# Replanning a fused sparse-attention and FFN kernel: DMA modelled as one stream, loads timed from need, fewer pairs on TensorE

## The chip, the cores and the metric

The kernel runs on one core of a Trainium2 chip. The metric is the device time of one execution in microseconds (us). Runs come in rounds, each with the kernel before beside the other on the same chip. "Fast" and "slow" are the states of an execution; here one is called slow when it is over 1.5% above the fastest of the same kernel. A median given below is of all runs.

The engines are PE (TensorE; PEld is its weight load), DVE (VectorE), ACT (ScalarE), POOL (GpSimd) and SP (which here mostly issues DMA). "Granted clock" is the share of TensorE's full clock in a stretch.

## The reference

Block-sparse attention over 4 batches and 8 heads of 768 tokens with 64 features, then a gated convolutional feed-forward part (FFN):

```python
scores = q @ k.T / 8
mask   = near_diagonal | first_and_last_block | sampled_blocks      # blocks of 32 tokens
x      = softmax(where(mask, scores, -1e9)) @ v                     # heads side by side: [4, 768, 512]
h      = maximum(x @ w_in, 0)                                       # [4, 768, 1024]
conv   = sum(conv_w[k] * shift(h, k - 1) for k in range(3))         # along the tokens
out    = (h * sigmoid(conv)) @ w_out                                # [4, 768, 512] float32
```

Inputs and outputs are float32; the kernel computes in bfloat16.

## The kernel before

The work is cut into 16 *pairs* (two heads of one batch) and 8 *halves* (384 tokens of one batch, all heads). Each pair's q and k are loaded by GpSimd's queue into `nat`, transposed so that the features lie on partitions, and copied by DVE into a slot `et`/`ot`. The first six pairs are transposed on TensorE. The others go through a DMA transpose into `tmp`:

```python
NSLOT = 6
NPE = 6                                   # pairs 0..5 on TensorE
...
t0 = op({"SP": 1.3}, xp(0), due - 8, [lq], alloc=tb, uses=[nb], lat=TLAT)     # DMA transpose of q
t1 = op({"SP": 1.3}, xp(1), due - 8, [lk], uses=[nb, tb], lat=TLAT)           # and of k, nat -> tmp
ce = op({"DVE": 0.5}, put(ET, 0), due, [t0, t1, slot_first.get(P - 1)], ...)  # et <- tmp
co = op({"DVE": 0.5}, put(OT, 64), due, [ce], uses=[slot_b[P], tb])           # ot <- tmp
```

Scores are TensorE matmuls into `st`; one exponential on ACT (`pt<-st`, 144 of them, each 1.04 us) takes eight blocks of 128x128; eight matmuls per exponential group multiply with v into `av`; DVE normalises (`xtok<-av`, 32 times), and a transpose gives `xT`, the input of the FFN. In the FFN TensorE multiplies (`mix<-xT,winb`), ACT or DVE applies the ReLU, DVE does the three multiplies and two adds of the convolution (`m<-hE`), ACT the tanh, DVE the gate, TensorE the output product. Half n's FFN runs while half n+1's attention does.

The order of all this is not written down. The kernel *declares* operations, each with the engines that may do it, a duration, a priority, its predecessors, a latency and its buffers; a list scheduler in the kernel then plans, while the program is being built, an order for each engine. `lat` of an operation is how long the planner believes its result takes to arrive. Twelve further passes re-plan, with priorities from the way back through the last plan:

```python
XLAT, TLAT = 3.908, 9.2201                # believed landing of xT's and tmp's transposes
PASSES = 12
...
def backward(self, order):                # priorities from the distance to the end
    ...
    for o, t in zip(order, end):
        o.prio = -t
        o.outs = []
        for b in o.allocs:
            b.index = None
            b.pool.holders = []           # o.start and o.end keep their old values

def run(self, passes):
    order = self.forward()
    for _ in range(passes):
        self.backward(order)
        order = self.forward()
    return order
```

Each engine executes its order strictly: one that reaches a copy whose transpose hasn't landed waits, whatever else stands behind (the profile after shows DVE do so for 8.71 us). Loads of later pairs were started at fixed times (`load_u`, as `earliest`). The mask rows of slots 2 to 5 were copied by DMA.

The softmax here doesn't subtract the row's maximum and nothing guards it: scores larger than these inputs give would overflow.

## Time and profile before

| | before |
|---|---|
| time, median of 3 | 215.12 us (215.08 to 215.75) |
| span of the profiled execution | 214.9 us (a fourth execution, of 216.58 us), mean granted clock 0.999 |
| busy DVE / PE / ACT | 189.7 / 198.8 / 182.1 us |
| attention ends (32nd normalisation starts) | 187.0 us |
| tail behind it | 27.9 us |

The prediction shows the busy table, the slices and the stretches. The granted clock in 40 slices, from the page (9 is 0.9 or more):

```profile
PEclk9999999999999999999999999999999999999999
```

The DMA transposes of q and k, from the DMA view, with the count and the median time from issue to landing in us:

```profile
tmp<-nat SPq DMA_TRANSPOSE x20, 6.5
```

There are two transposes for each of ten pairs, 20 in all. The 6.5 us needs care: the trace shows the landing of only 4 of the 20 (6.0 to 6.9 us), and the first of these 4 was issued at 52.1 us. The records of DMA packets cover the others. Each transpose into `tmp` moves 768 packets of 256 bytes and each into `xT` 384, and 20 x 768 + 27 x 384 = 25,728 is all that the trace has of this size. If the queue works them off in order, the transpose issued at 38.84 us, the first into `tmp`, began its last packet at 48.96 us, 10.1 us after its issue.

And the stretches, cut at the last normalisation of this execution, with busy us of PE, PEld, DVE, ACT, POOL, then granted clock, DMA share (packets of an engine overlap in time, so it can pass 1) and GB/s:

```profile
31.00:187.00 156.00, 149.48 (x2087) 117.20 (x2102) 147.64 (x415) 146.94 (x178) 56.09 (x128) 1.00 0.78 111
187.00:214.90 27.90, 22.76 (x119) 11.25 (x119) 22.20 (x65) 12.40 (x23) 6.03 (x14) 0.99 0.27 104
```

DVE is the third busy number. It idles 156.0 - 147.64 = 8.4 us in the middle and 27.9 - 22.20 = 5.7 us in the tail.

### The profile page before, as it was taken

The numbers are of one execution on the slowest core, as the hardware profiler recorded it, in microseconds if no ns is written. First come the engines' busy times: TensorE is split into PE (matmuls) and PEld (weight loads), VectorE is DVE, ScalarE is ACT, GpSimd is POOL, SyncE is SP. The second block draws the span as 40 slices with busy tenths as digits, with TensorE's granted clock in tenths as the row PEclk, the third lists the DMA queues.
The fourth block names the chain that finished last, engine by engine and source line by source line (L and its number), as shares of the span: only waits on it lengthen the run. The fifth ranks groups of instructions, "written<-read, shape, count | busy, mean of one in ns | idle before, by whom it ended". The sixth has DMA issues, their size and how long they took to land.

```text
span 214.9 us, 6588 instructions
## 1 busy us (share of the span) xinstructions
PE 198.8 (92%) x2579; PEld 150.4 (70%) x2596; DVE 189.7 (88%) x541; ACT 182.1 (85%) x227; POOL 81.8 (38%) x174
## 2 busy tenths in 40 slices
PE   7996999997999979999989999989999999998992
PEld 4785878886677857788768667667786787554441
DVE  6865627999989999479999999999999999999972
ACT  4595999999989989999998799989999999674541
POOL 8993414625505540446375302431241012443300
PEclk9999999999999999999999999999999999999999
DMA  6999994999999997899996993001110230022223
GB/s 170 152 177 204 199 203 61 142 154 134 190 136 212 150 119 80 148 146 213 168 136 106 129 204 107 18 20 62 59 23 21 71 116 21 18 98 101 99 98 146
DMA packets 50520, 25.84 MB, mean 120 GB/s; under 512 B 36321, under 2 KB 47353, under 8 KB 50489
## 3 DMA queue, kind: packets, MB, share of 16 engines
q0 software_dynamic: 18464, 11.14, 43.7%
q1 hardware_dynamic: 31592, 13.75, 31.6%
q10 hardware_dynamic: 432, 0.52, 0.7%
q8 instruction: 20, 0.33, 0.6%
q14 instruction: 12, 0.09, 0.2%
HBM read 23.08 MB, written 6.29 MB: 137 GB/s over the span
## 4 chain that ended last, share of the span: by engine, by line
DVE 59%; PE 15%; DMA 10%; ACT 6%; issue 5%; POOL 2%; SPq 1%; ACTq 0%; DVEq 0%; POOLq 0%
DVE m L753 19%; DVE m L759 10%; DVE hE L742 7%; PE st L678 6%; ACT pt L685 5%; DVE gT L781 5%; DVE xtok L631 5%; DMA nat<-in_k_dram 4%; DMA tmp<-nat 4%; PE mix L799 4%; DVE tn L772 3%; PE av L705 2%; DMA o2s<-in_q_dram 2%; DVE o2s L424 2%; PE st L799 2%
## 5 line engine op out<-in xcount | busy, mean ns | idle before, releaser
L685 ACT ACTIVATE pt<-st 128x1024 bf16<-128x1024 f32 x144 | 141.8, 1039 | 8.5 <-PE st L678 7.2
L705 PE MATMUL av<-vt,pt 128*128 128x65 bf16 x1152 | 57.9, 193 | 1.9 <-DVE vt L519 1.4
L753 DVE TENSOR_SCALAR m<-hE,cw 128x384 bf16<-128x384 bf16 x192 | 56.9, 346 | 0.2
L705 PEld LDWEIGHTS <-pt 128*128 128x128 bf16 x1152 | 50.4, 97 | 6.2 <-issue 1.7
L729 PE MATMUL mix<-xT,winb 128*128 128x384 bf16 x240 | 48.1, 325 | 1.9 <-DVE hE L742 1.1
L829 POOL COPY hE<-hE 128x254 bf16<-128x254 bf16 x32 | 18.4, 575 | 74.7 <-DVE hE L742 51.0
L799 PE MATMUL mix<-woutb,gT 128*128 128x512 bf16 x151 | 41.0, 379 | 2.4 <-DVE gT L781 1.6
L678 PE MATMUL st<-ot 88*128 88x128 bf16 (+1 forms) x224 | 42.5, 234 | 0.5 <-ACT pt L685 0.2
L678 PE MATMUL st<-et,ot 88*128 88x128 bf16 (+1 forms) x224 | 42.5, 234 | 0.1
L678 PE MATMUL st<-et 88*128 88x128 bf16 (+1 forms) x208 | 40.7, 239 | 1.7 <-ACT pt L685 1.7
L678 PEld LDWEIGHTS <-ot 88*128 88x128 bf16 x448 | 34.5, 97 | 10.1 <-issue 0.9
L678 PE MATMUL st<-ot,et 88*128 88x128 bf16 (+1 forms) x208 | 40.7, 239 | 0.7 <-ACT pt L685 0.4
L678 PEld LDWEIGHTS <-et 88*128 88x128 bf16 x416 | 32.3, 97 | 9.9 <-issue 3.3
L759 DVE TENSOR_TENSOR m<-m 128x768 bf16<-128x768 bf16 x64 | 35.1, 554 | 0.1
L769 ACT ACTIVATE tn<-m 128x768 bf16<-128x768 bf16 x32 | 27.7, 866 | 5.5 <-DVE m L759 5.4
L729 PEld LDWEIGHTS <-winb 128*128 128x128 bf16 x256 | 22.1, 97 | 13.1 <-issue 2.7
L799 PEld LDWEIGHTS <-gT 128*128 128x128 bf16 x200 | 16.5, 98 | 15.5 <-DVE gT L781 3.1
L742 DVE TENSOR_SCALAR hE<-mix 128x384 bf16<-128x384 f32 x37 | 20.2, 548 | 3.9 <-PE mix L729 3.8
L781 DVE TENSOR_TENSOR gT<-tn,hE 128x768 bf16<-128x768 bf16 x32 | 17.9, 562 | 0.1
L631 DVE TENSOR_TENSOR xtok<-av,rcp 128x384 bf16<-128x384 f32 x32 | 17.6, 549 | 0.3
L492 POOL DMA_DIRECT2D vn<-in_v_dram x16 | 11.9, 743 | 10.4 <-DVE vt L519 8.7
L830 POOL COPY hE<-hE 128x254 bf16<-128x254 bf16 x32 | 15.3, 479 | 0.0
(76 smaller groups left out, 168.7 us busy)
## 6 DMA issues: line engine op xcount, KB each, us to landing
out_dram<-o2s SPq DMA_DIRECT2D x23, 256.0 KB, 2.2
vn<-in_v_dram POOLq DMA_DIRECT2D x16, 192.0 KB, 6.2
nat<-in_q_dram POOLq DMA_DIRECT2D x15, 192.0 KB, 7.3
nat<-in_k_dram POOLq DMA_DIRECT2D x15, 192.0 KB, 6.4
winb<-in_moe_w_in_dram POOLq DMA_DIRECT2D x2, 512.0 KB, 12.2
woutb<-in_moe_w_out_dram POOLq DMA_DIRECT2D x2, 512.0 KB, 9.5
xT<-xtok SPq DMA_TRANSPOSE x27, 8.8
o2s<-in_k_dram ACTq DMA_DIRECT2D x2, 192.0 KB
```

Of the source, the lines that this page charges most:

```text
L631: nm = op({"DVE": 0.475}, lambda e: nc.vector.tensor_tensor(out=xtok_t[xk.index].rearrange("p c h d -> p h c d"), in0=o_of()[:, :, :, 0:64 ...
L678: nc.tensor.matmul(out=st_t[stb.index][:, 128 * x:128 * (x + n_)], lhsT=QK[kc % 2][s][0:88, 1, hh, kc // 2, :], rhs=QK[par][s][0:88, 0, hh ...
L685: e_op = op({"ACT": t_act(1024)}, lambda e, stb=stb, ptb=ptb: nc.scalar.activation(out=pt_t[ptb.index], in_=st_t[stb.index], func=AF.Exp, ...
L705: nc.tensor.matmul(out=av_t[av_buf[(n, P % 4)].index][:, off:off + 65], lhsT=pt_t[ptb.index][:, 128 * x:128 * x + 128], rhs=VT[P % NSLOT][ ...
L729: nc.tensor.matmul(out=tiles[hb.index][:, 0:384], lhsT=winb[:, fc, 128 * ffc:128 * ffc + 128], rhs=xT_t[xt_buf[n].index][:, fc, :], start= ...
L742: nc.vector.tensor_scalar(out=dst, in0=src, scalar1=0.5, scalar2=0.0, op0=ALU.mult, op1=ALU.max)
L753: nc.vector.tensor_scalar(out=m_t[cb.index][:, slot, o0:o1], in0=src, scalar1=w, scalar2=None, op0=ALU.mult)
L759: nc.vector.tensor_tensor(out=m[:, 0], in0=m[:, 0], in1=m[:, 1], op=ALU.add)
L769: th = op({"ACT": 0.745}, lambda e: nc.scalar.activation(out=tn_t[cb.index], in_=m_t[cb.index][:, 0], func=AF.Tanh, bias=0.0, scale=0.5), ...
L781: nc.vector.tensor_tensor(out=o, in0=t, in1=h, op=ALU.mult)
L799: nc.tensor.matmul(out=acc()[:, 0:o1 - o0], lhsT=gT_t[gb.index][:, ffc, 128 * c:128 * c + 128], rhs=woutb[:, ffc, o0:o1], start=(ffc == 0) ...
L829: nc.gpsimd.tensor_copy(out=h[:, f0:f0 + 2, 1:128], in_=h[:, f0:f0 + 2, 384:511])
```

## The change

The intent is a better plan: the planner counts every DMA on one shared stream (`DQ`) instead of giving each a private latency; loads begin 12 us ahead of need (`AHEAD`), read from the last plan; an engine may hold back up to 0.1 us for more urgent work (`PATIENCE`); four pairs stay on TensorE instead of six; mask rows go to DVE; one slot, one conv buffer and some FFN tiles are saved. All in one diff, cut to what matters (`...` marks cuts):

```diff
-FLEX = 0.0345
+FLEX = 0.054174241888482536
+PATIENCE = {"PE": 0.1, "ACT": 0.06768420072847306, "DVE": 0.002812048423731589}
...
-                    k = (s, o.prio, o.key)
+                    k = (max(s, t + PATIENCE.get(e, 0.0)), o.prio, o.key)
...
+        span = max(o.end for o in order)
         for o, t in zip(order, end):
             o.prio = -t
+            if o.ahead is not None:
+                o.earliest = span - t - o.ahead
             o.outs = []
+            o.start = o.end = None
...
-    NSLOT = 6
-    NPE = 6
+    NSLOT = 5
+    WIDE = ()
+    AHEAD = 12.0
+    NPE = 4
...
-    XLAT, TLAT = 3.908, 9.2201
+    XLAT, TLAT = 3.9296133203668684, 1.0
...
-    PASSES = 12
+    PASSES = 9
...
+    def sp_dma(fn, sp, dur, prio, deps, lat, alloc=None, uses=(), by="SP"):
+        i_ = op({by: sp}, fn, prio, deps, lat=0.1, alloc=alloc, uses=uses)
+        return op({"DQ": dur}, None, prio, [i_], lat=lat, uses=list(uses) + ([alloc] if alloc else []))
...
-            elif s == 1:
-                m[s] = op({"DVE": 0.58}, rows_by(t[s], t[0]), T(4.5 * s) - 2.5, [m[0]])
-            else:
-                m[s] = op({"SP": 0.46}, rows_to(t[s], t[0]), T(4.5 * s) - 6, [m[0]], lat=6.0,
-                          earliest=T(18 + 2 * s) if s > 3 else 0.0)
+            else:
+                m[s] = op({"DVE": 0.58}, rows_by(t[s], t[0]), T(4.5 * s) - 2.5, [m[0]])
...
-            t0 = op({"SP": 1.3}, xp(0), due - 8, [lq], alloc=tb, uses=[nb], lat=TLAT)
-            t1 = op({"SP": 1.3}, xp(1), due - 8, [lk], uses=[nb, tb], lat=TLAT)
+            t0 = sp_dma(xp(0), 1.25, 1.1, due - 8, [lq], TLAT, alloc=tb, uses=[nb])
+            t1 = sp_dma(xp(1), 1.25, 1.1, due - 8, [lk], TLAT, uses=[nb, tb])
...
-        xtr[(n, hp)] = op({"SP": 1.25}, tr, due - 5, [nm], lat=XLAT, uses=[xk] + us, alloc=al)
+        xtr[(n, hp)] = sp_dma(tr, 1.2, 0.8, due - 5, [nm], XLAT, uses=[xk] + us, alloc=al)
```

Left out: the same treatment of loads and stores, three conv buffers made two, the tanh written back into the conv buffer, batch-wide FFN tiles, other tuned offsets.

## The prediction

> **What bounds the kernel now.** I read the page's busy table first, then the table by stretch of time, then the groups, the chain that ended last, and the DMA landings. The page's head, its busy table and its slices:
>
> ```profile
> PE 198.8 (92%) x2579; PEld 150.4 (70%) x2596; DVE 189.7 (88%) x541; ACT 182.1 (85%) x227; POOL 81.8 (38%) x174
> ...
> PE   7996999997999979999989999989999999998992
> PEld 4785878886677857788768667667786787554441
> DVE  6865627999989999479999999999999999999972
> ACT  4595999999989989999998799989999999674541
> ...
> DMA  6999994999999997899996993001110230022223
> ```
>
> Three engines lie within 17 us of each other, so no single one explains the 215 us. The slices show where they are loose: DVE (VectorE) is loose in the first eight slices (to about 40 us) and around 85 us; the DMA engines are near full for the first 125 us and nearly empty after. I cut the trace at the points where this changes. Columns are busy us of each engine in the stretch, granted clock, DMA share and GB/s:
>
> ```profile
> 0.00:31.00 31.00, 26.52 (x376) 21.90 (x377) 19.83 (x63) 22.80 (x28) 19.65 (x32) 1.00 1.15 183
> 31.00:42.00 11.00, 11.00 (x173) 9.43 (x173) 8.63 (x22) 10.25 (x12) 5.12 (x12) 1.00 0.86 118
> 42.00:80.00 38.00, 34.79 (x512) 28.07 (x514) 37.12 (x104) 36.01 (x42) 17.24 (x34) 1.00 1.27 153
> 80.00:100.00 20.00, 19.90 (x292) 15.99 (x293) 15.56 (x44) 18.98 (x24) 6.22 (x13) 1.00 1.11 137
> 100.00:187.60 87.60, 84.39 (x1118) 63.89 (x1124) 86.93 (x251) 81.86 (x104) 27.51 (x71) 1.00 0.48 84
> 187.60:215.00 27.40, 22.16 (x116) 11.07 (x117) 21.60 (x63) 12.25 (x22) 6.03 (x14) 0.99 0.28 106
> ```
>
> 187.6 us is where the last attention output is normalised. DVE's idle time is 31.0 - 19.8 = 11.2 us in the start, 2.4, 0.9, 4.4, 0.7, and 5.8 in the tail. So from 42 us DVE is solid but for 80 to 100 us, where TensorE is (19.90 of 20). In the tail DVE runs without a gap to 208.3 us; then 6.6 us remain for the last output matmuls, the copy out and the store. The chain of waits says the same by share:
>
> ```profile
> DVE 59%; PE 15%; DMA 10%; ACT 6%; issue 5%; POOL 2%; SPq 1%; ACTq 0%; DVEq 0%; POOLq 0%
> ```
>
> The kernel is a start of some 31 us in which little but attention and loading runs, then 177 us in which DVE is the bound with one hole (80 to 100), then the closing 6.6 us.
>
> **What the Trainium skill says.** "Perfetto Trace Analysis", section "Identifying the Most-Contended Engine", takes occupancy as a fair measure for Vector and Scalar and not for matmuls; I therefore lean on DVE's 99% in 100 to 187.6 us and distrust TensorE's 96%. The trace agrees in part: eight attention-output matmuls count 0.41 us in the timeline, though the next kind begins 0.24 us after the first of them. The same page, "Optimization Strategy", says regimes with different limits may gain from interleaving; the hole at 80 to 100 us is such a regime. "DMA: Bandwidth & Descriptors", "Issuing engines are not separate DMA queues", has all queues run on the same 16 engines; the trace agrees: the two big queues take 43.7% and 31.6% of them, and the transposes of xtok land after 2.3 to 8.8 us. "VectorE: DVE Perf Modes", "Why PSUM operands drop a tier", says a PSUM source is slower per element; the groups agree: 768 elements from PSUM take about as long as 1536 from SBUF.
>
> ```profile
> L539 DVE COPY ot<-mix 64x768 bf16<-64x768 bf16 x12 | 6.7, 559 | 0.2
> L424 DVE COPY ot<-tmp 64x1536 bf16<-64x1536 bf16 x10 | 5.8, 580 | 0.3
> L424 DVE COPY et<-et 24x1536 bf16<-24x1536 bf16 x1 | 0.8, 758 | 0.0
> ```
>
> **The change, part by part.** I compared the static order of instructions of both kernels, engine by engine; it has counts and places and no time. Most of the diff (two conv buffers for three, batch-wide tiles for h and the gate, the tanh written into the conv buffer) changes no count: the wide path is switched off, so each engine does the same convolution in the same sizes.
>
> 1. *Four pairs on TensorE instead of six.* Pairs 4 and 5 now go through the DMA transpose. TensorE loses 24 transposes; six in a row took 0.49 us in the chain, so about 2 us. DVE loses 8 copies from PSUM (8 x 0.55 = 4.4 us) and gains 4 from SBUF (4 x 0.58 = 2.3 us). These stood at 36 to 45 us, where DVE is filling up: 2.1 us less on the path. Cost: four more DMA transposes at 20 to 35 us.
>
> 2. *Mask rows copied by DVE instead of DMA.* With 5 slots for 6, eight DMAs of 72 KB go; six copies of 24x1536 come (6 x 0.76 = 4.5 us). In the static order all six stand before the first FFN work, thus in the start with its 11.2 us of idle DVE. I count them as hidden. They free the queue of 6 x 72 KB, issued at 7.6 to 12 us, just ahead of a load of k issued at 11.27 us that took 8.96 us and is on the chain. ScalarE lost 3.1 us to scores between 10 and 31 us; I give this part 0.5 to 1 us.
>
> 3. *Balance of DVE and ScalarE.* DVE takes 3 more ReLUs (3 x 0.47 us, its spacing in the chain = 1.4 us) and one output copy less (0.6 us): +0.8 us on DVE; ScalarE gets about 1 us less.
>
> 4. *The sum on DVE.* Total: +4.5 - 4.4 + 2.3 + 0.8 = +3.2 us, so near 193 us busy. But of it +4.5 us (masks) and 1.2 us (pair 4's copies, now ahead of the FFN) fall into the start. After about 31 us there remains 189.7 - 19.8 = 169.9 us before, and 169.9 + 3.2 - 5.7 = 167.4 us after: 2.5 us less on the bound.
>
> 5. *Planner: one DMA stream, loads timed from need, patience.* No count changes, only order. It can only win by closing idle time: DVE's after 31 us and before the tail is 2.4 + 0.9 + 4.4 + 0.7 = 8.4 us. The new order does move FFN work: at the eighth normalisation 22 of the 192 multiplies stand ahead in both, but the first ones come a pair earlier (6 instead of 2 by the fifth). Behind the last attention output stand 104 output and 36 input matmuls of the FFN where it was 94 and 32. At their spacing in the timeline (0.217 and 0.163 us) that is 10 x 0.217 + 4 x 0.163 = 2.8 us of TensorE moved into the tail, and DVE's tail gains 6 multiplies, a gate, an add-one, less one ReLU: 6 x 0.24 + 0.47 + 0.27 - 0.47 = 1.7 us. So attention should end about 6 us earlier, and the tail be about 2 us longer. I credit 2 of the 8.4 us of idle as recovered; this is my choice, because TensorE bounds part of the hole.
>
> Sum: 2.5 us (work off the bound) + 0.5 (start) + 2.0 (idle recovered) = 5.0 us; less about 0.4 us for new waits on the transposes. 215.1 - 4.6 = **210.5 us**.
>
> **Rivals.**
> *The hole is only moved, nothing recovered.* For it: TensorE is 19.9 of 20 in the hole and the sum of its work falls by only 2 us. Against: in 42 to 80 us it idles 3.2 us and in 100 to 187.6 another 3.2. Then 2.5 to 3 us stay: 212.5 us.
> *A DMA wait takes the place.* The planner's lag for the tmp transposes falls from 9.2 to 1.0 us beyond their turn on the stream; this trace has them land after 6.5 us. Engines run in order, and pair 4's copies stand between the third and fourth copies of xT, at about 28 us. If its transposes land late, DVE stalls, the normalisation behind it stalls, and the FFN starts late. For it: DMA share 1.15 in the start. Against: the masks' DMAs are gone and the loads are spread over the span. It would cost 2 to 4 us: 213 to 215 us.
> *Conv buffers too few.* Two in place of three may leave DVE waiting on the tanh (0.87 us, behind an exponential of 1.04 us). Against: another pair's multiplies and adds, 2.7 us, fit into that wait. If it binds, 32 pairs x 0.1 us: 213 us.
> *The plan works fully.* If 6 of the 8.4 us go: 206.5 us.
>
> **Range and chances.** The outcomes run from 206.5 (all idle closed) to 214.5 us (gain eaten by DMA waits); eight in ten lie there. Two per cent is 4.3 us, so the line is 210.8 us, close to my middle: faster 0.54, within 2% 0.40, slower 0.06, because a loss needs new waits above all that is saved.
>
> **What would show it.** Right: DVE busy near 193 us, with 24 to 26 us by 31 us; tmp copies x12 and six more 24x1536 copies; last attention normalisation near 181 us, tail near 29 us; DMA slices no longer full to 125 us and above 1 later; DVE idle between 42 us and the tail under 5 us. Wrong: DVE waits named tmp<-nat or et<-tmp over 1 us; DVE waits on tanh; the first FFN multiply later than 34 us; an attention end not before 185 us. I would be wrong low if these waits appear, and wrong high if TensorE and DVE both stay above 97% from 42 us on.

## More of the kernel before

The clock is high in every slice.

The timeline of DVE, just where the later reading turns (start, duration, line, operation, and in brackets the idle time before it and what ended it):

```profile
24.57 0.36 DVE L424 COPY xT<-mix 128x384 bf16<-128x384 bf16 x1 [0.44 <-PE mix L644]
...
27.20 0.36 DVE L424 COPY xT<-mix 128x384 bf16<-128x384 bf16 x1 [0.56 <-PE mix L644]
...
30.74 0.36 DVE L424 COPY xT<-mix 128x384 bf16<-128x384 bf16 x1 [0.60 <-PE mix L644]
```

DVE waits here in small pieces, each for TensorE (the row of transposes in `mix`); no copy of pair 4 or 5 stands between.

## The result, and the profile after

The median was 227.01 us (224.45 to 227.8, 4 runs), against 215.1 us before in the same rounds. The ratio is 1.0544, with a 95% interval of 1.0462 to 1.0625: slower by 5.4%. A ratio is the mean time of one kernel's fast runs over that of the other's fast runs of the same rounds, so not quite the ratio of the medians quoted. The kernel's output is right.

The profiled execution is the fastest of the four (224.45 us; span 222.7 us, clock 0.985), while the profiled one of the kernel before (216.58 us) is slower than its median. So the two profiles lie 7.8 us apart and the medians 11.9: some 4 us of the usual loss are in neither profile. Three of the five executions of the kernel after, at 227.4 to 227.8 us, had a mean clock of 0.977; no trace of these is kept. The page of the profiled one has the busy table, the slices and the chain:

```profile
PE 200.6 (90%) x2572; PEld 150.5 (68%) x2572; DVE 191.7 (86%) x546; ACT 182.1 (82%) x225; POOL 81.2 (36%) x170
...
PE   6997905999899999999898999899999999899992
...
DVE  6999404799989999539999999999999999999962
...
PEclk9999985999999999999999999999999999999999
DMA  7999999956999993994968699510200231221233
...
DVE 46%; PE 25%; DMA 11%; issue 7%; POOL 6%; ACT 4%; SPq 0%; DVEq 0%; ACTq 0%; POOLq 0%
```

Against the lines of before, the totals barely moved: DVE 191.7 for 189.7 us, PE 200.6 for 198.8, ACT the same. What is new is a pit (a slice is 5.6 us): DVE is at 4, 0 and 4 tenths in slices five to seven, PE at 0 and 5 in six and seven, where the clock is at 8 and 5; DVE's loose place near 88 us stands near 95 us now. New too is less DVE and more PE on the chain. The waits name it (engine, line, what it waited for: total us, times, longest):

```profile
ACT pt L699 <- PE st L692: 14.2, 15, 8.1
DVE et L434 <- DMA tmp<-nat: 11.7, 3, 8.7
...
PE mix L657 <- DVE xtok L640: 7.6, 1, 7.6
```

On DVE's timeline the first wait for a transpose stands between a copy of `xT` and the next one:

```profile
24.25 0.61 DVE L434 COPY xT<-mix 128x384 bf16<-128x384 bf16 x2
33.57 0.55 DVE L434 COPY et<-tmp 64x1536 bf16<-64x1536 bf16 x1 [8.71 <-DMA tmp<-nat]
34.05 0.34 DVE L434 COPY xT<-mix 128x384 bf16<-128x384 bf16 x1
```

This is pair 4's copy. DVE stood for 8.71 us, from 24.86 to 33.57 us. It could not do the `xT` copy or the normalisation behind it, so TensorE had nothing to transpose (7.6 us), and ACT no scores (8.1 us). How late the four transposes of this time came, from issue, and what the chain before it was (start, duration, what):

```profile
DMA to landing us min/median/max: 8.8/10.7/12.7
```

```profile
14.72 6.07 DMA nat<-in_k_dram
20.80 12.67 DMA tmp<-nat
```

So the load of k ended at 20.8 us and its transpose took another 12.7 us to land; the median is 4.3 us, of the 19 of 24 whose landing the trace shows. The packets say where the time went. Taken in order as above, the transpose of q (issued at 18.11 us) began its packets from 22.21 to 28.27 us and landed at 29.07; that of k began its own from 28.27 to 32.84 us. So over half of k's 12.7 us, 7.5 us, went by before its first packet, for the most part on q's turn. The 768 packets took 6.1 and 4.6 us here; for the transpose issued at 48.47 us, with no load beside it, they took 1.1 us. (Why q's first packet came only 4.1 us after its issue, where it came after 1.2 us at 48.47, is not shown.)

What they shared the DMA engines with: packets begun, per stretch. In these stretches a transpose packet took 31 ns (median; 18 ns over the whole run), a weight packet 96 to 98 ns.

| us | weight packets of 1024 B | other load packets, 384 or 768 B | transpose packets of 256 B |
|---|---|---|---|
| 21 to 24 | 462 | 0 | 141 |
| 24 to 27 | 440 | 0 | 450 |
| 27 to 30 | 404 | 89 | 481 |
| 30 to 33 | 6 | 542 | 464 |

From 24 us on there is about one packet of the transposes for each packet of the loads: first of the weights, then, when these are through, of the next q and k. So a transpose gets one small packet for each larger one of the other queue. The Trainium skill, page "DMA: Bandwidth & Descriptors", section "Queues, rings and completion order", says that each DMA engine goes round robin between the rows that have work, a packet at a time; the counts agree with such a turn, if each packet of the trace is one turn. In the kernel before no transpose of this kind was issued before 38.8 us.

The gap also costs afterwards. The same four FFN matmuls, as the first after the gap and some 2 us later:

```profile
37.41 1.47 PE L743 MATMUL mix<-xT,winb 128*128 128x384 bf16 x4
...
39.68 0.81 PE L743 MATMUL mix<-xT,winb 128*128 128x384 bf16 x4
```

The Trainium skill, page "TensorE: Matmul & The Clock Gate", section "Part 1: The HAM clock gate", says that TensorE's clock halves after an idle window of about 3.4 us and returns after a busy one. The trace agrees: after 7.55 us of idling the granted clock was 0.66 on the mean of 30 to 40 us (the trace has it at half from 32.1 to 38.9 us), and the matmuls took 1.47 for 0.81 us. An empty gap is not needed, though: e5 below shows a fall without one.

Milestones of both executions, in us from the first instruction:

| | before | after | after - before |
|---|---|---|---|
| 19th exponential starts | 28.7 | 26.3 | -2.4 |
| 25th | 35.0 | 41.3 | +6.3 |
| 49th | 62.7 | 68.8 | +6.1 |
| 97th | 123.6 | 127.9 | +4.3 |
| 139th | 177.6 | 182.0 | +4.4 |
| last normalisation | 187.0 | 191.4 | +4.4 |
| end | 214.9 | 222.7 | +7.8 |

(The 2.4 us at the 19th can't be claimed for the change: a mere other order of the kernel before shows 26.6 there.) The stretches, as cut for before:

```profile
0.00:31.00 31.00, 25.14 (x372) 21.38 (x372) 21.80 (x66) 23.14 (x28) 22.02 (x34) 1.00 1.18 167
31.00:191.40 160.40, 148.96 (x2063) 116.04 (x2064) 145.29 (x410) 144.18 (x171) 52.58 (x117) 0.98 0.71 110
191.40:222.70 31.30, 26.51 (x139) 13.04 (x137) 24.63 (x72) 14.74 (x27) 6.62 (x20) 1.00 0.28 101
```

With DVE's busy and idle time this makes an account of the whole span, 7.8 us:

| DVE, us | before | after | difference |
|---|---|---|---|
| busy in all | 189.7 | 191.7 | +2.0 |
| idle, 0 to 31 | 11.2 | 9.2 | -2.0 |
| idle, 31 to the last normalisation | 8.4 | 15.1 | +6.7 |
| idle in the tail | 5.7 | 6.7 | +1.0 |

The wait of 8.71 us lies in two rows of it: 6.1 us before 31, 2.6 us after.

### The profile page after: what moved, and what is told of

It is laid out like the page before. It is cut to its first block, busy times and chain, and to the rows that moved or that the text cites. A ratio compares the mean times of both kernels' runs of the same rounds, so it can differ in the third digit from the quotient of the medians.

```text
span 222.7 us, 6575 instructions
## 1 busy us (share of the span) xinstructions
PE 200.6 (90%) x2572; PEld 150.5 (68%) x2572; DVE 191.7 (86%) x546; ACT 182.1 (82%) x225; POOL 81.2 (36%) x170
## 4 chain that ended last, share of the span: by engine, by line
DVE 46%; PE 25%; DMA 11%; issue 7%; POOL 6%; ACT 4%; SPq 0%; DVEq 0%; ACTq 0%; POOLq 0%
DVE m L775 17%; PE st L692 9%; DVE m L781 8%; DMA tmp<-nat 8%; PE mix L813 7%; DVE hE L756 6%; PE av L719 4%; PE mix L743 4%; DVE xtok L640 4%; DVE gT L794 3%; ACT pt L699 3%; DMA nat<-in_k_dram 3%; DVE m L792 3%; POOL nat L497 2%; DVE ot L434 2%
## 5 line engine op out<-in xcount | busy, mean ns | idle before, releaser
L699 ACT ACTIVATE pt<-st 128x1024 bf16<-128x1024 f32 x144 | 139.7, 1033 | 15.1 <-PE st L692 14.2
L851 POOL COPY hE<-hE 128x254 bf16<-128x254 bf16 x64 | 31.7, 523 | 79.0 <-DVE hE L756 67.9
L719 PE MATMUL av<-vt,pt 128*128 128x65 bf16 x1152 | 55.6, 193 | 1.2 <-DVE vt L528 1.2
L743 PE MATMUL mix<-xT,winb 128*128 128x384 bf16 x240 | 49.1, 328 | 3.3 <-DVE hE L756 2.8
L813 PE MATMUL mix<-woutb,gT 128*128 128x512 bf16 x168 | 43.7, 379 | 2.5 <-DVE gT L794 1.3
L692 PE MATMUL st<-et 88*128 88x128 bf16 (+1 forms) x208 | 41.3, 240 | 0.6 <-ACT pt L699 0.5
L692 PEld LDWEIGHTS <-et 88*128 88x128 bf16 x416 | 32.1, 97 | 8.3 <-issue 1.6
L790 ACT ACTIVATE m<-m 128x768 bf16<-128x768 bf16 x32 | 27.3, 853 | 6.8 <-DVE m L781 6.7
L813 PEld LDWEIGHTS <-gT 128*128 128x128 bf16 x200 | 17.6, 98 | 17.8 <-DVE gT L794 3.3
L756 DVE TENSOR_SCALAR hE<-mix 128x384 bf16<-128x384 f32 x41 | 22.4, 547 | 3.4 <-PE mix L743 3.3
L794 DVE TENSOR_TENSOR gT<-m,hE 128x768 bf16<-128x768 bf16 x32 | 17.7, 555 | 0.2
L434 DVE COPY et<-tmp 64x1536 bf16<-64x1536 bf16 x12 | 6.7, 555 | 11.7 <-DMA tmp<-nat 11.7
```

Source lines behind the costliest of these rows:

```text
L692: nc.tensor.matmul(out=st_t[stb.index][:, 128 * x:128 * (x + n_)], lhsT=QK[kc % 2][s][0:88, 1, hh, kc // 2, :], rhs=QK[par][s][0:88, 0, hh ...
L699: e_op = op({"ACT": t_act(1024)}, lambda e, stb=stb, ptb=ptb: nc.scalar.activation(out=pt_t[ptb.index], in_=st_t[stb.index], func=AF.Exp, ...
L719: nc.tensor.matmul(out=av_t[av_buf[(n, P % 4)].index][:, off:off + 65], lhsT=pt_t[ptb.index][:, 128 * x:128 * x + 128], rhs=VT[P % NSLOT][ ...
L743: nc.tensor.matmul(out=tiles[hb.index][:, 0:384], lhsT=winb[:, fc, 128 * ffc:128 * ffc + 128], rhs=xT_t[xt_buf[n].index][:, fc, :], start= ...
L756: nc.vector.tensor_scalar(out=dst, in0=src, scalar1=0.5, scalar2=0.0, op0=ALU.mult, op1=ALU.max)
L790: th = op({"ACT": t_act(w) + 0.055}, lambda e: nc.scalar.activation(out=m_of(1), in_=m_of(0), func=AF.Tanh, bias=0.0, scale=0.5), due + 2. ...
```

## The experiments

**Theory A**: pair 4's and then pair 5's copies come up in DVE's order before their transposes have landed; DVE waits, and everything behind it; TensorE's gap lowers its clock, which adds to it. **Rivals**: the transfer of the output weights alone makes it late (A1); the rest of the plan is worse by itself, whatever the transposes do; the planner's reset is to blame; the wait only displaces idle time that was there anyway. The expectations name their theories in their own words and letters. Eighteen kernels ran. They come here in three groups, not in order of time. All had their result checked; two failed it.

### Group 1: the wait itself

**e1_copies_later.** Pair 4's two copies are moved behind, to just before the transposes of pair 6, in the finished order. Nothing else moves.

```diff
...
-        for o in sc.run(PASSES):
+        order = sc.run(PASSES)
+        for o in put_ops[4][2:]:
+            order.remove(o)
+        at = order.index(put_ops[6][0].deps[0])
+        order[at:at] = put_ops[4][2:]
+        for o in order:
```

> The changed kernel with only two DVE instructions moved in the order: the copies of pair 4's transposed tiles (et<-tmp and ot<-tmp) stand 26 rows later, just before the transposes that reuse their buffer. No transfer and no count changes. Theory A (DVE waits in order for a late transpose, and that is all the loss): the 8.7 us wait goes, the granted clock stays at 1.0 between 30 and 40 us, and the time falls by 9 to 12 us, to 213 to 217 us. Rival B (the loss lies in the other parts: fewer conv buffers, five slots, longer tail): it stays above 221 us. Rival C (the wait only moves to the next copy or to the scores of pair 4): DVE or TensorE show a new wait over 4 us and the time is 218 to 223 us.

Measured: 222.53 us, ratio 1.0346 (1.0296 to 1.0396), some 4.5 us less than the kernel after. The waits of this run:

```profile
DVE et L434 <- DMA tmp<-nat: 5.0, 3, 2.1
```

The total fell from 11.7 to 5.0 us and the longest from 8.7 to 2.1. A later pair's transpose now lands last: its row on the chain begins at 36.09 us and is 12.73 us long. TensorE stood once, for 3.79 us until 50.53 us, and the clock was 0.83 in 50 to 60 us. The position of pair 4's copies did cost, and the lateness isn't special to pair 4. But theory A's 213 to 217 us were missed: the wait of 8.7 us is gone and three fifths of the loss remain.

**e2_wout_later.** Only the two issues of the output weights are moved, behind the loads of pair 7.

```diff
...
+        late = [w[0] for w in wout_is]
+        for o in late:
+            order.remove(o)
+        at = order.index(k_iss[7]) + 1
+        order[at:at] = late
```

> The changed kernel with only the two issues of the output weights moved behind the loads of pair 7, as late as the second of them stands in the kernel before. DVE's order is untouched. Theory A1 (the transposes of pair 4 are late because 2 MB of output weights were issued at 17 and 19 us onto the same engines): pair 4's second transpose lands 4 to 8 us sooner than its 12.7 us, the wait falls from 8.7 to 1 to 4 us, and the time to 216 to 221 us. Rival A2 (the transposes are slow beside any loads, or start too late): the landing stays over 10 us, the wait over 7 us and the time over 222 us.

Measured: 224.22 us, 1.0436 (1.038 to 1.0492). The longest wait was still 7.9 us and the landing 11.9 us. So the output weights alone are not the cause; the next loads take their place on the engines. The packets show it: against 580 and 648 packets of the transposes in 24 to 27 and 27 to 30 us stand 576 and 634 of loads, of all kinds together, again one to one.

**e5_both_later.** As e1, but pair 5's copies too (before the transposes of pair 7, or before their first use if that comes earlier).

> The changed kernel with the DVE copies of pair 4 moved as in the first experiment and those of pair 5 moved behind the following 14 rows as well, just ahead of their first use by the scores. The first experiment moved the 8.7 us wait to pair 5 (its second transpose took 12.7 us to land, 36.1 to 48.8 us). Theory A (only the place in DVE's order is wrong; the data come early enough for TensorE): no DVE wait over 2 us before 60 us, 214 to 218 us. Rival D (the DMA engines are full until about 50 us and pair 5's tiles come later than the scores of pair 5 can wait): the wait stays or turns into a wait of the scores, 219 to 223 us.

Measured: 221.07 us, 1.0278 (1.0238 to 1.0318). No wait for `tmp` is left before 60 us (one of 2.4 us later). The clock still fell once, to 0.83 in 50 to 60 us, though no gap of TensorE from 40 to 80 us was longer than 1.3 us: it was busy 2.25 us of the 3.4 us before the fall. (The expectation says that e1 had moved the 8.7 us wait to pair 5; the longest that e1 left was 2.1 us.) Moving the copies by hand gets back half of the loss.

**e6_no_dma_need.** The copies into `et` and `ot` read a tile of zeros and so need no transpose, which runs as before and is not read. Same instructions in the same order, but for one clearing of that tile. (The result still passed within tolerance, presumably since the scores are so small that softmax hardly depends on them. So the check of the result says little about q and k, and this kernel is wrong by design all the same.)

```diff
+    flat_t = many(1, [128, 2, 2, 3, 128], BF16, "flat")[0]
...
+                nc.vector.memset(flat_t, 0.0)
...
-                return lambda e, s=s, tb=tb: copy_to(e, t[s][0:64], tmp_t[tb.index][r0:r0 + 64])
+                return lambda e, s=s, tb=tb: copy_to(e, t[s][0:64], flat_t[r0:r0 + 64])
```

> WRONG RESULT ON PURPOSE: the changed kernel with every copy from a transposed tile reading a constant tile of zeros of the same shape instead; all loads and transposes are still issued, the order is the planner's own, one memset of 0.4 us is added. It is the plan without its DMA waits on transposes. If the prediction's sum was right but for these waits: 209 to 213 us. If the rest of the change brings nothing: 214 to 217 us. If the loss lies elsewhere: above 219 us.

Measured: 217.43 us, 1.011 (1.0064 to 1.0156), clock 0.997. So the need for the transposes in time, with all that follows from it, is worth 227.0 - 217.4 = 9.6 of the 12 us by the medians, from different rounds (6.6 us between the profiled spans; the profiled run of the kernel after was its fastest, that of e6 its slowest). What is left, 1.1%, is not a wait for a transpose. Its stretches:

```profile
0.00:31.00 31.00, 27.21 (x392) 22.57 (x393) 26.07 (x73) 23.39 (x29) 21.35 (x34) 1.00 1.16 167
31.00:184.80 153.80, 145.21 (x2031) 113.85 (x2044) 143.54 (x404) 144.18 (x171) 52.07 (x117) 1.00 0.77 115
184.80:216.10 31.30, 26.42 (x137) 13.03 (x137) 24.63 (x72) 14.74 (x27) 6.63 (x20) 0.98 0.28 101
```

DVE did 26.07 us of work by 31 us, 6.2 more than before: the start took the extra work, as predicted. But DVE's idle time from there to the last normalisation was 153.8 - 143.54 = 10.3 us, where it was 8.4; and the tail grew to 31.3 us with 6.7 us of idling.

**e15_after_filler.** The kernel after, with 60 matmuls on a constant tile put ahead of the matmul that waits for the late copies, to keep TensorE busy in the gap.

```diff
             def tr(e):
+                for x in range(60 if n == 0 and hp == 3 else 0):
+                    nc.tensor.matmul(out=tiles[mb.index][:, 0:256], lhsT=warm[:, 0:128], rhs=warm[:, 0:256],
+                                     start=True, stop=True)
```

> The kernel after with 60 matmuls of constant tiles (128x256) put ahead of the first matmul that waits for the late transposes, so that TensorE is busy for most of the 7.5 us gap from 27.8 to 35.8 us. Nothing else moves. Theory A with the clock as a second cost: granted clock 1.00 in 30 to 40 us instead of 0.66, the four matmuls at 37 us take about 0.8 us and not 1.47, and the time falls by 1.5 to 3 us against the kernel after (224 to 225.5). Rival (the lower clock is a bystander, the wait is all of the cost): clock restored, but time within 0.7 us of the kernel after.

Measured: 224.86 us (one of four runs slow), 1.0424 (1.0359 to 1.0489). The stretch of 30 to 40 us, first of the kernel after, then of this run:

```profile
30.00:40.00 10.00, 4.20 (x35) 3.21 (x36) 3.04 (x7) 1.53 (x2) 1.45 (x2) 0.66 1.38 173
```

```profile
30.00:40.00 10.00, 9.96 (x108) 8.46 (x105) 3.16 (x8) 3.16 (x5) 1.45 (x2) 1.00 1.43 174
```

The granted clock is 1.00 where it was 0.66, and the four matmuls of 1.47 us:

```profile
37.49 0.81 PE L746 MATMUL mix<-xT,winb 128*128 128x384 bf16 x4
```

From the release of the waiting transpose to the 25th exponential it took 40.7 - 36.6 = 4.1 us, in the kernel after 41.3 - 35.8 = 5.5. So the clock is worth about 1.4 us here, on top of the wait, by one profile of each. By the whole time the gain is 2.1 us of medians, but from different rounds and with intervals that overlap, and the profiled span wasn't shorter (223.2 us; its first exponential came 1.7 us later, at 9.7 for 8.0 us, before anything that was changed). The local reading carries this, not the total.

### Group 2: what the planner believes, and how many pairs need it

**e4_tlat.** Only the believed lag of the transposes is set back.

```diff
-    XLAT, TLAT = 3.9296133203668684, 1.0
+    XLAT, TLAT = 3.9296133203668684, 9.2201
```

> The changed kernel with only the planner's lag of a transposed load put back to the 9.2 us of before (from 1.0); still four pairs on TensorE. Theory A (the plan's belief about the transposes is the fault): pair 4's copies stand 7 rows later and their loads are issued earlier in the order, so the wait falls under 4 us and the time to 212 to 218 us. Rival (the static order is too coarse to help; DMA traffic decides): the wait stays over 6 us, time above 221 us.

Measured: 222.56 us (219.24 to 227.2; two of four runs slow), 1.0263 (1.0164 to 1.0363). The wait for `tmp` fell from 11.7 to 0.4 us. The wait moved: 7.5 us of DVE for first-FFN matmuls (seven waits), 2.1 us of PE for `xT`, and a clock of 0.83 in 60 to 70 us. The short lag causes the wait that was seen; a longer lag alone doesn't bring the time back (its two fast runs took 219.24 and 221.91 us).

**e9_measured_dma.** The planner is given durations close to what the packets of the traces show (a load of q 1.63 us of all 16 engines, of k or v 1.26, of weights 3.14), and a lag of 6. Lines cut:

```diff
-    XLAT, TLAT = 3.9296133203668684, 1.0
+    XLAT, TLAT = 3.9296133203668684, 6.0
-     ... P, 1.25,    ... 1.1, [iq],    ... 1.1,    ... 2.7, gate=v_iss[3]
+     ... P, 1.65,    ... 1.3, [iq],    ... 1.3,    ... 3.3, gate=v_iss[3]
```

> The changed kernel planned with slower transfers, near what the traces show when the engines are full: loads of q 1.65, of k and v 1.3, of weights 3.3 us of the stream (from 1.25, 1.1, 2.7), and a lag of 6.0 us for a transposed load (from 1.0). In the order, pair 4's copies now stand at row 100 of DVE instead of 66. Theory E (the new plan is right but believes the transfers too fast): no DVE wait on tmp<-nat over 2 us, 212 to 217 us. Rival F (any new plan of this kernel costs 1 to 2% against the tuned one, waits on transfers or not): 217 to 220 us.

Measured: 227.94 us, 1.0587 (1.0509 to 1.0665): no better than the kernel after. A wait of 5.4 us for `tmp` stayed, and DVE waited 9.6 us in all for `av` (six waits, the longest 2.4 us). Better averages did not make a better plan. That the tuned numbers only fit the plan that they were tuned for is a guess that this run agrees with.

**e3_npe5** and **e8_after_npe6.** Five and six pairs on TensorE (`NPE = 5`, `NPE = 6`), with all else as after.

> The changed kernel with pair 4 put back on TensorE (5 pairs instead of 4), planned anew. Theory A: without pair 4's transposes no copy from tmp stands ahead of the FFN's start; no DVE wait over 3 us in the first 60 us, 211 to 216 us. Rival B: the time stays above 221 us. Rival C: pair 5's copies wait in its place, DVE shows a wait on tmp<-nat over 3 us, 216 to 221 us.

> The changed kernel with six pairs on TensorE as before, planned anew; no DMA transpose before pair 6. Rival D (transposes of pairs 4 and 5): the start is as in the kernel before or 2 us ahead, no wait on tmp<-nat before 60 us, 211 to 216 us. If the re-planning itself brings new waits, as with five pairs (225.8 us, where TensorE's granted clock fell to 0.56 between 50 and 60 us): above 219 us.

Measured: 225.79 us (1.0519) and 224.99 us (1.0473). With five, no wait for `tmp` remained, but DVE waited 9.3 us for first-FFN products (nine waits, the longest 2.1 us), and the clock fell to 0.56 in 50 to 60 us. With six, the wait came back on a later pair, in 60 to 70 us:

```profile
DVE et L434 <- DMA tmp<-nat: 7.4, 1, 7.4
```

So not the four pairs as such: with six, the short lag plants the wait on a later pair, and with five, other waits cost as much.

**e17_npe6_tlat** and **e18_npe6_tlat6.** Both set back together: six pairs, lag 9.22 (and 6.0).

> The kernel after with six pairs on TensorE and the planner's lag of the transposes back at 9.22, both as before; everything else of the change stays. Theory A (the loss is late transposes and what follows them, and the rest of the change is small): 213 to 218 us, no wait on tmp over 1 us, clock 0.99 or more in every stretch. Theory P (the one stream, the loads timed from need or the patience cost time of themselves): 220 us or more, with waits that neither the kernel before nor the kernel without need of the copies shows.

> The same with the lag at 6.0, near the landing time of 6.5 us that the trace of the kernel before shows. Theory A: a wait on tmp of at most 3 us and 214 to 221 us, between the run of six pairs alone with the short lag (225 us) and the run with the long lag. If the time is as long as with the short lag (224 us or more) and the stall is back, a lag that is right on the median is not enough. If it is as fast as the long lag, the exact lag does not matter.

Measured: 220.96 us (219.6 to 224.14; one of four runs slow), 1.0273 (1.0194 to 1.0353), and 221.74 us, 1.032 (1.0272 to 1.0369). With the long lag no wait of DVE or TensorE for `tmp` is left, and the profiled execution has a clock of 1.0. Theory A expected 213 to 218 us and missed. The other theory expected new waits, and there are none over 5 us. The stretches (profiled run: the fastest, span 217.9 us) show where the time is:

```profile
31.00:185.70 154.70, 148.31 (x2072) 115.28 (x2070) 143.34 (x402) 144.29 (x174) 51.81 (x116) 1.00 0.75 109
185.70:217.90 32.20, 26.54 (x138) 12.73 (x136) 26.36 (x77) 13.73 (x25) 6.68 (x21) 1.00 0.27 98
```

Attention ends at 185.7 us, 1.3 earlier than before. The tail is 32.2 us, with 26.4 us of DVE work against 22.2. So here too the new plan pays attention's lead back in the tail, and more. With e6 this suggests that the rest of the change costs some 1 to 3% even without a late transpose. With the lag of 6.0, too, DVE waits for no transpose; so the exact lag made little difference here.

### Group 3: from the side of the kernel before

**e7_before_npe4.** The kernel before with `NPE = 4` only.

> The kernel before with only the number of pairs on TensorE put from 6 to 4, planned by its own planner (lag 9.2 us, its own load times). Rival D (four more DMA transposes in the first 50 us are the cost, whatever the plan): 220 to 226 us with DVE or the scores waiting on tmp<-nat before 60 us. Theory A (the new plan's place of the copies is the cost): 213 to 218 us.

Measured: 218.3 us, 1.0153 (1.0114 to 1.0191). No wait for `tmp`: with the long lag the old planner places the copies late enough. The clock fell to 0.70 in 70 to 80 us. By the groups the copies into `et` and `ot` cost DVE 22.7 us for 24.7, so the saving of 2 us that the prediction worked out is there. DVE's busy total is 189.6 us for 189.7 all the same, since the planner dealt other work anew (two more output copies, four fewer ReLUs, the copies of v slower), and the time is longer. Four pairs are no gain by themselves.

**e12_before_flex.** A null test: another order of the same work, by the new `FLEX` alone.

> A second null change: the kernel before with only the planner's margin for giving a copy to ScalarE put to the changed kernel's 0.054 (from 0.0345). Rival F: 217 to 220 us. If orders are about equal: 213 to 217 us.

Measured: 214.38 us, 0.9965 (0.9898 to 1.0031). Another order needn't cost anything.

**e10_before_passes11.** Meant as a second null test, 11 passes for 12.

> A null change: the kernel before with 11 passes of its planner instead of 12. Same work, same counts, another order (some 240 lines of difference on DVE, half of its order moved). It measures what another order alone is worth. Rival F (the order of before is a lucky or tuned one): 217 to 220 us. If orders of this planner are about equal: 213 to 217 us.

Measured: 222.25 us, 1.0341, but the result was **wrong** (relative error 0.33), so its time counts for nothing. The planned order held the fault: an operation that overwrote a buffer had been put ahead of the last reader of the old contents. `backward` leaves last pass's `end` in place, and the planner asks `u.end is None` to see whether a reader has been planned yet. A check of each planned order for this finds two such places each in e10 and in e11, and none in the kernel before or after, nor in e7, e12, e13, e14 and e16.

**e11_before_masks_dve.** The kernel before with the mask rows on DVE.

> The kernel before with only the mask rows of slots 2 to 5 copied by DVE instead of DMA (eight copies of 24x1536, 6 us of DVE, in the start). The prediction held them hidden and the freed DMA worth 0.5 to 1 us: 213 to 216 us, the scores of unit 19 about 1 to 2 us sooner than the 28.7 us of before. If they are on the path: 217 to 221 us.

Measured: 220.47 us, 1.0229, and again **wrong** (0.318), by the same fault. Inconclusive; e16 repeats it with the reset added, and is right.

**e13_before_reset** and **e14_after_stale.** The mending line alone in the kernel before, and taken out of the kernel after.

```diff
             o.outs = []
+            o.start = o.end = None
             for b in o.allocs:
```

> The kernel before with only the planner's reset of start and end times. Theory A (the time is lost to late transposes of the pairs moved off TensorE, and the clock drop after): six pairs stay on TensorE, no transpose is needed before 45 us, so this is only another order of the same work: within 1.5% of before (212 to 218 us), no wait on tmp over 1 us before 60 us, clock 0.99 or more. Theory R (the reset makes plans slower whatever the transposes do): 219 us or more, with a wait that the kernel before does not have.

> The kernel after with the reset taken out. Theory A: pair 4's and pair 5's copies still need transposes by about 30 us, so a wait on tmp of 3 us or more before 50 us stays and the time stays at 222 to 228 us. Theory R: the time comes back to 218 us or less, without such a wait.

Measured: 216.39 us, 1.0052 (0.9997 to 1.0107), right; and 229.48 us, 1.0641 (1.0575 to 1.0707), with a wait of 9.6 us for `tmp`. The reset costs about half a per cent (1.1% at most by the interval), and its absence doesn't help. It isn't the cause. It was needed for safety.

**e16_before_reset_masks.** The kernel before with the reset and the mask rows on DVE.

```diff
+            o.start = o.end = None
...
-            elif s == 1:
-                m[s] = op({"DVE": 0.58}, rows_by(t[s], t[0]), T(4.5 * s) - 2.5, [m[0]])
             else:
-                m[s] = op({"SP": 0.46}, rows_to(t[s], t[0]), T(4.5 * s) - 6, [m[0]], lat=6.0,
-                          earliest=T(18 + 2 * s) if s > 3 else 0.0)
+                m[s] = op({"DVE": 0.58}, rows_by(t[s], t[0]), T(4.5 * s) - 2.5, [m[0]])
```

> The kernel before with the reset and the mask rows copied by VectorE. Against the run of the reset alone. The prediction's step: six copies of 0.76 us hidden in the start, the freed transfers worth 0.5 to 1 us: 0.5 to 1 us faster than the reset alone. Rival (the copies stand in front of work on VectorE in the start and are not hidden): 1 to 4 us slower, with VectorE's share of 0 to 31 us up by 4.5 us and its later work as much as before.

Measured: 216.86 us, 1.0074 (1.0026 to 1.0121), right. First 31 us of the reset alone, then of this run:

```profile
0.00:31.00 31.00, 27.39 (x404) 23.33 (x405) 20.27 (x64) 24.30 (x29) 19.89 (x32) 1.00 1.16 188
```

```profile
0.00:31.00 31.00, 26.05 (x385) 22.09 (x386) 25.77 (x71) 23.24 (x28) 19.77 (x32) 1.00 1.16 174
```

DVE did 25.77 us of work by 31 us where it did 20.27, and the time is the same within the intervals. The copies are hidden, as predicted; a gain of 0.5 to 1 us from the freed transfers isn't to be seen.

### What stays open

Against the expectations: theory A was right about the place and the waits and mostly wrong about the time. e1, e3, e4, e5, e8 and e9 (where its kind of claim has other letters), e17 and, by less than 1 us, e7 and e18 came out above the range that it gave them; e14 did too, though it kept the wait. e6 lies 0.4 us above the range for "the rest brings nothing", e16 in neither of its ranges. Only e13 and e15 met both the range and the signs, and e2 met its rival A2. So that the late transposes are all of the loss does not hold.

No version here beat the kernel before beyond doubt; e12 is 0.35% ahead with an interval that includes none. Whether the tail can be kept short in the new plan, and why the runs of e17 spread over 4.5 us, was not settled: only its fastest was profiled. That the loads delay the transposes rests on the packet counts, on the 1.1 us that a transpose's packets take alone, and on e2 (other loads took the place of the one moved away). A run with all weight loads away was not made, as the FFN needs them.

## Why the prediction was wrong

It said 210.5 us, a range of 206.5 to 214.5, and 6% for slower by over 2%. It came to 227.0.

**The step that failed first: "less about 0.4 us for new waits on the transposes".** The mechanism was in the text, as the rival "A DMA wait takes the place", with the place (pair 4's copies between the third and fourth copies of `xT`), the time (28 us) and the sign (the lag that falls from 9.2 to 1.0). The size was not: it worked with a landing of 6.5 us, "this trace has them land after 6.5 us". That is the median of 4 of the 20 transposes, all issued after 52 us. The same trace had warnings nearer to the start: an `xT` transpose issued at 35.87 us landed after 8.8 us, the end of the range that the prediction itself quotes, and the first `tmp` transpose took 10.1 us to its last packet. In the change's place they landed after 8.8 to 12.7 us, two in a row on one queue, each sharing the engines with the loads packet for packet. It also left out that a gap this long lowers TensorE's clock. The rival was given 2 to 4 us; the wait alone was 8.7, the clock 1.4 more, the whole by e6 9.6 us of medians (6.6 of profiled spans). The argument against it ("the masks' DMAs are gone and the loads are spread") looked at bytes removed, 0.6 MB. The full DMA engines of that stretch (share 1.15 before, 1.18 after) it named on the other side, but gave them no price.

**The planner: "recover 2 of 8.4 us".** e6, where no transpose is waited for, has 10.3 us of idle DVE there: 1.9 more and not 2.0 less. The hole stayed: at 80 to 90 us DVE was busy 6.46 of 10 us in e6, 7.51 before. The prediction's own first rival had said so, with TensorE as the reason; there TensorE was busy 9.50 of 10 us and ACT 9.41, and no run shows which of them bounds it.

**"2.5 us less on the bound after 31 us".** In e6 DVE's work after 31 us was 143.5 + 24.6 = 168.1 us, for 147.6 + 22.2 = 169.8: 1.7 less. Right in kind.

**The start, 0.5 us.** Not seen (e16), though the copies are hidden as it said.

**"Tail about 2 us longer".** 3.4 us in the kernel after and in e6 alike (31.3 for 27.9): DVE's work 2.4 more instead of 1.7, and 1.0 us of idling that it had not counted. Attention was to end 6 us earlier; without the waits (e6) it ended 2.2 earlier, with them 4.4 later.

The sum for e6, in profiled spans: -1.7 (work) + 1.9 (idle in the middle) + 1.0 (idle in the tail) = +1.2 us, from 214.9 to 216.1. The sum of the prediction without its waits was -5.0. The waits bring the other 6.6 us, to 222.7.

**What was right.** DVE's total (191.7 for "near 193"); the counts of copies; the list of signs for being wrong ("DVE waits named tmp<-nat", "an attention end not before 185 us"). The chances were wrong in their shape: a plan for engines that execute strictly in order had several ways to lose 5 us and few to gain so much, and 6% for a loss did not say that. It also missed the mended fault, which e13 and e14 show to be no part of the time.

## What to carry to other kernels

When operations run in a fixed order, price a new dependency by how late it lands *where it will stand*, with the traffic of that stretch, and not by its median elsewhere; then add the work behind it on every engine, and the clock after the gap. A plan that frees work on the busiest engine wins nothing unless the idle time falls too: split busy and idle by stretch and see where the difference goes. DVE's busy total said nothing of the outcome here: 191.7 us at a span of 222.7 us, 194.2 at 216.1. A median of landings is worth what it counts: ask how many landings it is of, and when. And check a schedule's order for buffers that are overwritten before they are read: a planner's left-over state shows up as a wrong result only in some plans.

## What the Trainium skill lacked or had wrong

- "DMA: Bandwidth & Descriptors", "Queues, rings and completion order": it has the turn-taking between rows, but no figure for what a transpose suffers from it. Here the 768 packets of a transpose took 1.1 us with no load beside them, and 6.1 and 4.6 us beside 873 and 798 packets of loads. From issue to landing it was 2.7 us at best and 12.7 us at the worst in one run, the latter with another transpose ahead in its queue.
- "DMA: Bandwidth & Descriptors", same section: it speaks of a packet as about 9 to 17 descriptors. What this trace calls a packet has 256 to 1024 bytes, and their counts are close to one for one (440 and 450 in 3 us). Whether the engine switches after each or after several can't be told from such counts.
- "TensorE: Matmul & The Clock Gate", "Part 1: The HAM clock gate": agrees for a long gap (1.47 for 0.81 us after 7.55 us of idling, and a filler of 60 matmuls kept the clock at 1.00). But its idle window need not be empty: in e5 the clock fell at 55.6 us though TensorE had been busy 2.25 of the 3.4 us before, in e7 at 69.15 us after 1.64 of 3.4, with no gap over 1.3 us. It gives no figure for how much work such a window may hold, nor the price in a kernel with several busy engines: about 1.4 us here for one gap.
